# A fused attention and mixer kernel: its order taken from a list plan instead of generators and tile pools

## The chip, the cores and the metric

The kernel runs on one core of a Trainium2 chip. The metric is the device time of one execution in microseconds (us). The engines are TensorE (PE, with PEld for its weight loads), VectorE (DVE), ScalarE (ACT), GpSimd (POOL) and SyncE (SP). POOL issues the loads, which convert float32 to bfloat16 on the way; SP issues the stores.

## The reference

There are 8 batches of 576 positions, 8 heads of 64, and a model width of 512.

```python
scores = scale * q @ k^T + slope[h] * -(i - j)        # where 0 <= i - j < 128, else -1e9
x = softmax(scores) @ v                               # heads side by side: [8, 576, 512]
u = x + (relu(x^T @ w_tok1) @ w_tok2)^T               # token mix: 576 -> 256 -> 576
out = u + relu(u @ w_ch1) @ w_ch2                     # channel mix: 512 -> 1536 -> 512
```

## The kernel before, in words

576 positions are four blocks of 128 and a remainder of 64. Two batches form a pair `pr`: blocks 0 to 3 are the even batch, 4 to 7 the odd one, and the two remainders share block 8, `TAIL`, one in partitions 0 to 63 and one in 64 to 127. A block has a q, a k and a v tile, 1,024 rows of 64 numbers each (512 for half of TAIL).

Attention of a block: `transposes` (L199, copied by DVE at L205 into `qkT`), `scores` (L225: 64-row matmuls, even and odd heads in the two row halves of the array), an Exp on ACT (L234), `mask` on DVE (L245), `values` (L266, reciprocal L269, normalising multiply L271) into `xb`. A window of 128 makes each block need its own keys and those of the block before.

`token_mix` of a batch: two accumulations `t1` over the batch's four blocks (L314) and its 64 remaining rows (L318, 64-row matmuls), relu on ACT (L332), then for each block `ht` (L348), an add on DVE (L349), `ut` transposes (L354) and a copy (L360). For odd batches there is also TAIL, whose weights `W2t` are padded with zeros to 128 columns for each of its halves. `channel_mix`: 12 `ct` groups of four matmuls (L446) with relu on ACT (L448), for odd batches 3 `cx` groups for TAIL (L455), then for each block an accumulation `o2` of 12 matmuls (L464) in four pieces, an add (L468) and a store.

The order: `opening` writes out batch 0's attention and token mix by hand, with matmuls on zeros (`spin`) between. After that `interleave` alternates channel mix b with `side(b + 1)`, which is the attention and token mix of the next batch, by costs in nanoseconds that generators yield:

```python
interleave(main, other, 0.78 if b else 1.4)
drain(other)
```

So `side` advances 0.78 of what the channel mix does, and what is left of it is drained. The tile scheduler orders the other engines and POOL's and SP's queues. POOL's order at the start is: blocks 0 to 3 and half of TAIL, W1, W2, WC1 in four parts, WC2 in four parts, W2t, blocks 4 to 7, the other half of TAIL, and from there one block for each `transposes` of a later one. PSUM has 8 banks: the scores take two pairs, `ps_o` has one (tp, ot, ut), `ps_m` three (t1, ht, ct, cx, o2).

Of the kernel before, what the change touches and what calls it, by code (L numbers as in the profile page):

```python
# [12 lines left out]
F32 = mybir.dt.float32  # L13


@with_exitstack
def kernel(
# [37 lines left out]
    ld = ctx.enter_context(tc.tile_pool(name="ld", bufs=12))  # L55
    tpool = ctx.enter_context(tc.tile_pool(name="tp", bufs=8))
    ppool = ctx.enter_context(tc.tile_pool(name="pp", bufs=3))
    small = ctx.enter_context(tc.tile_pool(name="small", bufs=4))
    xpool = ctx.enter_context(tc.tile_pool(name="xp", bufs=2))
    rpool = ctx.enter_context(tc.tile_pool(name="rp", bufs=2))  # L60
    opool = ctx.enter_context(tc.tile_pool(name="op", bufs=3))
    rawp = ctx.enter_context(tc.tile_pool(name="raw", bufs=2))
    PS = bass.MemoryType.PSUM
    ps_s = [ctx.enter_context(tc.tile_pool(name=f"ps_s{e}", bufs=1, space=PS)) for e in range(2)]
    ps_o = ctx.enter_context(tc.tile_pool(name="ps_o", bufs=1, space=PS))
    ps_m = ctx.enter_context(tc.tile_pool(name="ps_m", bufs=3, space=PS))

    ident = const.tile([P, P], BF16, name="ident")

    dist = const.tile([P, 2, P], F32, name="dist")  # L70

    NV = 14
    vring = [const.tile([P, H, D + 1], BF16, name=f"v{i}") for i in range(NV)]
    made = {"v": 0}
# [9 lines left out]
    loaded = {}  # L84

    def tiles(pr, blk):
        got = {"q": ld.tile([P, H, D], BF16, name="qld", tag="qld"),
               "k": ld.tile([P, H, D], BF16, name="kld", tag="kld"),
               "v": vring[made["v"] % NV]}
        made["v"] += 1  # L90
        loaded[pr, blk] = got
        return got

    def fetch(got, parts):
        for name, t in (("q", q), ("k", k)):
            for b, s0, n, p0 in parts:
                nc.gpsimd.dma_start(out=got[name][p0 : p0 + n, :, :], in_=rows(t, b, s0, n))  # L97
        for b, s0, n, p0 in parts:
            nc.gpsimd.dma_start(out=got["v"][p0 : p0 + n, :, 0:D], in_=rows(v, b, s0, n))  # L99


    ORDER = [0, 1, 2, 3, 7, TAIL, 4, 5, 6]
    todo = [(pr, blk) for pr in range(1, B // 2) for blk in ORDER]

    def load_next(n):
        for _ in range(n):
            if todo:
                key = todo.pop(0)
                fetch(tiles(*key), parts_of(*key))


    zero = const.tile([P, DM], BF16, name="zero")
    nc.vector.memset(zero[:, :], 0.0)
    for t in vring[0:5]:
        nc.vector.memset(t[:, :, D : D + 1], 1.0)
    raws = []
    for name, t, eng in (("q", q, nc.sync), ("k", k, nc.scalar)):
        raw = rawp.tile([P, H, D], F32, name="raw", tag="raw")
        eng.dma_start(out=raw[:, :, :], in_=rows(t, 0, 0, P))
        raws.append(raw)  # L120
# [7 lines left out]

    tiles(0, 0)
    tiles(0, 1)  # L130
    for name, t in (("q", q), ("k", k)):
        nc.gpsimd.dma_start(out=loaded[0, 1][name][:, :, :], in_=rows(t, 0, P, P))
    for blk in (0, 1):
        nc.gpsimd.dma_start(out=loaded[0, blk]["v"][:, :, 0:D], in_=rows(v, 0, blk * P, P))
    for blk in (2, 3):
        fetch(tiles(0, blk), parts_of(0, blk))
    last = tiles(0, TAIL)
    for name in ("q", "k"):
        nc.vector.memset(last[name][R:P, :, :], 0.0)
    nc.vector.memset(last["v"][R:P, :, 0:D], 0.0)  # L140
    fetch(last, parts_of(0, TAIL)[0:1])
    for t in vring[5:]:
        nc.vector.memset(t[:, :, D : D + 1], 1.0)


    masks = [const.tile([P, 4, 2, P], BF16, name=f"mask{e}") for e in range(2)]
    maskt = [const.tile([P, 4, 2, P], BF16, name=f"maskt{e}") for e in range(2)]
    for e in range(2):
        for i, h in enumerate(HEADS[e]):
            nc.scalar.activation(out=masks[e][:, i, :, :], in_=dist[:, :, :], func=ACT.Exp,  # L150
                                 scale=-float(slopes[h]))

    def tail_masks():

        for e in range(2):
            for i in range(2):
                nc.vector.tensor_copy(out=maskt[e][:, :, 0, i * R : (i + 1) * R],
                                      in_=masks[e][:, :, 0, 0:R])
            nc.vector.tensor_copy(out=maskt[e][:, :, 1, :], in_=masks[e][:, :, 1, :])
            nc.vector.memset(maskt[e][0:R, :, 1, R:P], 0.0)  # L160


    W1 = const.tile([P, NC + 1, DTOK], BF16, name="W1")
    W2 = const.tile([P, NJ, NC * P], BF16, name="W2")
    W2t = const.tile([P, 2, NJ, P], BF16, name="W2t")
    WC1 = const.tile([P, NCB, DCH], BF16, name="WC1")
    WC2 = const.tile([P, NHT, DM], BF16, name="WC2")
    nc.vector.memset(W2t[:, 0, :, R:P], 0.0)
    nc.vector.memset(W2t[:, 1, :, 0:R], 0.0)

    def load_weights():
        nc.gpsimd.dma_start(
            out=W1[:, 0:NC, :], in_=moe_w_tok1[0 : NC * P, :].rearrange("(c p) n -> p c n", p=P)
        )
        w2 = moe_w_tok2.rearrange("(j p) s -> p j s", p=P)
        for i in range(2):
            nc.gpsimd.dma_start(out=W1[i * R : (i + 1) * R, NC, :], in_=moe_w_tok1[NC * P : S, :])
        nc.gpsimd.dma_start(out=W2[:, :, :], in_=w2[:, :, 0 : NC * P])
        w = moe_w_ch1.rearrange("(j p) h -> p j h", p=P)
        for x in range(4):  # L180
            hs = slice(x * DCH // 4, (x + 1) * DCH // 4)
            nc.gpsimd.dma_start(out=WC1[:, :, hs], in_=w[:, :, hs])
        w = moe_w_ch2.rearrange("(j p) c -> p j c", p=P)
        for x in range(4):
            js = slice(x * NHT // 4, (x + 1) * NHT // 4)
            nc.gpsimd.dma_start(out=WC2[:, js, :], in_=w[:, js, :])
        for i in range(2):
            nc.gpsimd.dma_start(out=W2t[:, i, :, i * R : (i + 1) * R], in_=w2[:, :, NC * P : S])


    qkT = {}
    xs = {}

    def transposes(pr, blk, copy):
        got = loaded[pr, blk]
        tp = ps_o.tile([P, 2 * NHP, P], BF16, name="tp", tag="o")
        for i, t in enumerate(("q", "k")):
            for hp in range(NHP):
                nc.tensor.transpose(  # L199
                    tp[:, i * NHP + hp, :],  # L200
                    got[t][:, 2 * hp : 2 * hp + 2, :].rearrange("p h d -> p (h d)"),
                    ident[:, :],
                )
        t = tpool.tile([P, 2 * NHP, P], BF16, name="qkT", tag="qkT")
        copy(out=t[:, :, :], in_=tp[:, :, :])  # L205
        qkT[pr, blk] = t

    def scores(pr, blk, half=None):


        tail = blk == TAIL
        c0, c1 = (0, P) if half is None else (half * R, (half + 1) * R)
        first = 0 if tail or blk % NC else 1
        me = qkT[pr, blk]
        sp = [ps_s[e].tile([P, 4, 2, P], F32, name=f"sp{e}", tag="s") for e in range(2)]
        work = [(1, blk, c0, c1)]
        if tail:
            work += [(0, (j + 1) * NC - 1, j * R, (j + 1) * R) for j in range(2)
                     if half is None or half == j]
        elif not first:  # L220
            work += [(0, blk - 1, 0, P)]
        for i in range(4):
            for kind, kb, a, z in work:
                for e in range(2):
                    nc.tensor.matmul(  # L225
                        sp[e][:, i, kind, a:z],
                        lhsT=qkT[pr, kb][e * D : (e + 1) * D, NHP + i, :],
                        rhs=me[e * D : (e + 1) * D, i, a:z],
                        start=True, stop=True,
                    )  # L230
        pb = []
        for e in range(2):
            pe = ppool.tile([P, 4, 2, P], BF16, name=f"pe{e}", tag=f"pe{e}")
            nc.scalar.activation(out=pe[:, :, first:, c0:c1], in_=sp[e][:, :, first:, c0:c1],  # L234
                                 func=ACT.Exp, scale=scale)
            pb.append(pe)
        return pb

    def mask(blk, pb, half=None):
        tail = blk == TAIL  # L240
        c0, c1 = (0, P) if half is None else (half * R, (half + 1) * R)
        first = 0 if tail or blk % NC else 1
# [78 lines left out]
    def token_mix(b):  # L321
# [6 lines left out]
        for j in range(NJ):  # L328
            t1 = ps_m.tile([P, DM], F32, name="t1", tag="m")
            for c in range(NC + 1):  # L330
                mix_in(t1, half, j, c, xb)
# [216 lines left out]
```

## Time and profile before

| | |
|---|---|
| median of 3 runs | 337.15 us (335.84 to 337.27) |
| profiled execution | 337.96 us, span 336.2 us |
| PE busy | 310.6 us, 92% of the span |
| DVE, ACT, POOL busy | 173.3, 137.4, 110.4 us |
| mean granted PE clock | 0.971 |
| loads through POOL's queue | 115,648 packets, 17.7 MB |

Times are counted from the first instruction of the span. "Busy" sums an engine's instructions; matmul ends are modelled. The clock is the share of full speed that was granted to PE. In a timeline row the columns are start, duration, engine, line, operation, what it writes and reads, the count, and in brackets the idle time ahead of it with what ended it.

### The profile page before, as it was taken

To read this page: it belongs to the slowest core of one execution; us is meant where nothing else is said; L and a number is where in the kernel's file an instruction comes from. 1 tells how busy PE (TensorE), PEld (TensorE's weight loads), DVE (VectorE), ACT (ScalarE), POOL (GpSimd) and SP (SyncE) were. 2 spreads that over 40 slices of the span, in tenths; PEclk is the share of its full clock that TensorE was granted. 3 is DMA by queue.
4 is the path that set the end of the run, shared out by engine and by line. 5 is a ranking of instruction groups with operands and counts; after the bars stand their busy time and mean duration, and the time that the engine had idled before them with its cause. 6 is when DMAs were issued, how large, how long until landed. Compare 5 with 4: busy or idle time off the path is not lost.

```text
span 336.2 us, 6518 instructions
## 1 busy us (share of the span) xinstructions
PE 310.6 (92%) x2693; PEld 163.1 (49%) x2739; DVE 173.3 (52%) x394; ACT 137.4 (41%) x210; POOL 110.4 (33%) x141
## 2 busy tenths in 40 slices
PE   8877998677999999999999999999999999999993
PEld 3543454324655555455564555455664555455541
DVE  4865057643665646474656547464756447361021
ACT  5523754112764037503863047404772057304600
POOL 9873698899774033303572000000000000000000
PEclk9977999957999999999999999999999999999998
DMA  9999999999999269914999220011000120011022
GB/s 126 142 180 205 147 146 171 186 131 149 133 87 98 65 117 72 66 51 93 77 82 79 96 62 3 0 65 62 2 2 25 71 64 0 2 62 62 2 88 69
DMA packets 123005, 28.08 MB, mean 84 GB/s; under 512 B 113888, under 2 KB 118368, under 8 KB 122976
## 3 DMA queue, kind: packets, MB, share of 16 engines
q0 software_dynamic: 115648, 17.70, 74.2%
q1 hardware_dynamic: 6288, 9.70, 8.6%
q8 instruction: 21, 0.34, 0.4%
q10 hardware_dynamic: 1040, 0.26, 0.4%
q14 instruction: 8, 0.07, 0.1%
HBM read 35.91 MB, written 9.44 MB: 135 GB/s over the span
## 4 chain that ended last, share of the span: by engine, by line
PE 83%; DVE 7%; POOL 3%; issue 2%; ACT 2%; DMA 2%; POOLq 0%
PE o L464 28%; PE ct L446 22%; PE ot L266 6%; PE sp L225 5%; PE tp L199 5%; PE ht L348 5%; PE t L314 4%; PE ut L354 3%; PE cx L455 2%; DVE xb L271 2%; DVE pe L245 2%; DMA kld<-in_k_dram 2%; PE t L318 1%; ACT pe L234 1%; PE hh L422 1%
## 5 line engine op out<-in xcount | busy, mean ns | idle before, releaser
L448 ACT ACTIVATE r<-ct 128x512 bf16<-128x512 f32 x96 | 56.2, 601 | 124.5 <-PE ct L446 124.5
L464 PE MATMUL o<-WC,r 128*128 128x512 bf16 x367 | 94.3, 379 | 2.1 <-DVE ob L468 0.8
L446 PE MATMUL ct<-uT,WC 128*128 128x512 bf16 x366 | 93.3, 382 | 2.0 <-issue 0.8
L234 ACT ACTIVATE pe<-sp 128x1024 bf16<-128x1024 f32 (+1 forms) x74 | 63.2, 906 | 26.6 <-PE sp L225 26.6
L464 PEld LDWEIGHTS <-r 128*128 128x128 bf16 x384 | 35.2, 98 | 37.9 <-issue 4.6
L446 PEld LDWEIGHTS <-WC 128*128 128x128 bf16 x384 | 34.2, 98 | 30.5 <-issue 1.3
L97 POOL DMA_DIRECT2D qld<-in_q_dram x38 | 33.2, 875 | 46.3 <-PE tp L199 37.7
L468 DVE TENSOR_TENSOR ob<-o,ub 128x512 f32<-128x512 f32 x36 | 24.8, 689 | 45.6 <-PE o L464 44.2
L245 DVE TENSOR_TENSOR pe<-pe,mask 128x1024 bf16<-128x1024 bf16 (+1 forms) x66 | 39.5, 613 | 8.6 <-ACT pe L234 8.0
L205 DVE COPY qkT<-tp 128x1024 bf16<-128x1024 bf16 x37 | 25.6, 691 | 34.6 <-PE tp L199 34.6
L99 POOL DMA_DIRECT2D v<-in_v_dram x38 | 33.0, 883 | 15.8 <-PE ot L266 6.6
L266 PE MATMUL ot<-v,pe 128*128 128x65 bf16 (+1 forms) x552 | 29.8, 196 | 5.7 <-DVE xb L271 4.9
L97 POOL DMA_DIRECT2D kld<-in_k_dram x38 | 33.4, 883 | 5.0 <-DMA WC<-in_moe_w_ch_dram 3.5
L349 DVE TENSOR_TENSOR ub<-ht,xb 128x512 bf16<-128x512 f32 x32 | 21.6, 688 | 25.8 <-PE ht L348 25.4
L266 PEld LDWEIGHTS <-pe 128*128 128x128 bf16 (+1 forms) x552 | 21.8, 100 | 23.5 <-DVE xb L271 17.2
L271 DVE TENSOR_TENSOR xb<-ot,rt 128x256 bf16<-128x256 f32 (+1 forms) x74 | 31.4, 424 | 2.5
L269 DVE RECIPROCAL rt<-ot 128x4 f32<-128x4 f32 (+1 forms) x74 | 13.3, 179 | 25.1 <-PE ot L266 24.6
L225 PE MATMUL sp<-qkT 64*128 64x128 bf16 (+1 forms) x552 | 22.4, 214 | 2.3 <-DVE qkT L205 2.2
L225 PEld LDWEIGHTS <-qkT 64*128 64x128 bf16 x552 | 15.8, 94 | 17.4 <-DVE qkT L205 16.7
L314 PE MATMUL t<-xb,W 128*128 128x512 bf16 x59 | 18.6, 404 | 0.4 <-issue 0.4
L348 PE MATMUL ht<-r,W 128*128 128x512 bf16 x53 | 17.2, 416 | 0.4 <-ACT r L332 0.3
L360 DVE COPY uT<-ut 128x512 bf16<-128x512 bf16 x28 | 11.8, 422 | 8.2 <-PE ut L354 8.2
(67 smaller groups left out, 208.9 us busy)
## 6 DMA issues: line engine op xcount, KB each, us to landing
out_dram<-ob SPq DMA_DIRECT2D x32, 256.0 KB, 2.0
v<-in_v_dram POOLq DMA_DIRECT2D x32, 128.0 KB, 4.9
qld<-in_q_dram POOLq DMA_DIRECT2D x31, 128.0 KB, 4.8
kld<-in_k_dram POOLq DMA_DIRECT2D x31, 128.0 KB, 4.8
WC<-in_moe_w_ch_dram POOLq DMA_DIRECT2D x8, 384.0 KB, 11.9
out_dram<-ob SPq DMA_DIRECT2D x8, 128.0 KB, 2.3
qld<-in_q_dram POOLq DMA_DIRECT2D x8, 64.0 KB, 4.5
kld<-in_k_dram POOLq DMA_DIRECT2D x8, 64.0 KB, 4.2
```

The lines of the kernel that those rows point to most:

```text
L97: nc.gpsimd.dma_start(out=got[name][p0 : p0 + n, :, :], in_=rows(t, b, s0, n))
L99: nc.gpsimd.dma_start(out=got["v"][p0 : p0 + n, :, 0:D], in_=rows(v, b, s0, n))
L225: nc.tensor.matmul(sp[e][:, i, kind, a:z], lhsT=qkT[pr, kb][e * D : (e + 1) * D, NHP + i, :], rhs=me[e * D : (e + 1) * D, i, a:z], start=T ...
L234: nc.scalar.activation(out=pe[:, :, first:, c0:c1], in_=sp[e][:, :, first:, c0:c1], func=ACT.Exp, scale=scale)
L245: nc.vector.tensor_tensor(out=pb[e][:, :, first:, c0:c1], in0=pb[e][:, :, first:, c0:c1], in1=mk[:, :, first:, c0:c1], op=ALU.mult)
L266: nc.tensor.matmul(ot[to, i, :], lhsT=l, rhs=r, start=m == 0, stop=m == len(mms) - 1, skip_group_check=True)
L271: nc.vector.tensor_tensor(out=x4[r0:r1, :, e, :], in0=ot[r0:r1, :, 0:D], in1=rt[r0:r1, :, :].broadcast_to([r1 - r0, 4, D]), op=ALU.mult)
L314: nc.tensor.matmul(t1[:, :], lhsT=W1[:, c, j * P : (j + 1) * P], rhs=xb[:, half * NC + c, :], start=c == 0, stop=False)
L348: nc.tensor.matmul(ht[:, :], lhsT=l, rhs=r, start=n == 0, stop=n == len(mms) - 1)
L446: nc.tensor.matmul(ct[:, :], lhsT=WC1[:, cb, t * P : (t + 1) * P], rhs=uT[:, cb, :], start=cb == 0, stop=cb == NCB - 1)
L448: nc.scalar.activation(out=r2[:, t, :], in_=ct[:, :], func=ACT.Relu)
L464: nc.tensor.matmul(o2[:, :], lhsT=l, rhs=WC2[:, t, :], start=t == 0, stop=t == NHT - 1)
```

## The change

Every step becomes an operation of a `Plan`: an engine, a cost in nanoseconds, a rank, and the buffers that it makes, adds to, rewrites or reads. Buffers are placed in rings of fixed tiles. `plan.run()` is a list schedule at build time: at each turn it takes, over all engines, the operation that can start earliest (rank, then number, breaks ties), places its buffers in the slot that comes free first, and moves the engine's clock on. POOL's operations keep the order in which they were written. Then `emit` sorts everything by its planned start and writes it out; all five engines keep that order. In predicted gaps of PE over 500 ns in the first 60 us it puts matmuls on zeros into a bank that the plan has free.

- PSUM: four banks in one ring for tp, ot, ut, t1, ht, ct, cx and o2; the scores keep their two pairs.
- POOL's order: WC1, then blocks 4 to 7, W2t, the other half of TAIL, then WC2, then the later pairs.
- Ranks: `side(0)` ahead of everything, then `side(1)`, then channel mixes in turn, with `side(b + 1)` spread over 0.93 of channel mix b. Several batches' steps can mix.
- Opening: no order by hand; all four adds and all four uT copies go to DVE (ACT and an identity matmul had half).
- Token mix: `HOLD` makes the first t1 matmul wait for the batch's third block. TAIL's rows are copied by DVE into the other half of partitions (`xt`), so that t1 for j = 0 and j = 1 take different row halves; both `t1` banks are then held until TAIL's x is there.
- W2t loses its zero padding: 64 columns, written to output partitions 0 to 63 and 64 to 127.

The diff, cut to its core:

```diff
+SEM = 40.0
+SPREAD = 0.93
+class Plan:
...
+    def dma(self, emit, descs, packets, makes=(), rewrites=(), order=None):
+        o = self.op("POOL", 550 + 0.33 * descs, emit, 0, makes=makes, rewrites=rewrites,
+                    order=order or self.slot())
...
+    def run(self):
...
+        free = {"PE": 1500.0, "ACT": 5600.0, "DVE": 1600.0, "POOL": 2000.0, "SP": 1300.0}
+        server, lanes, sent = SERVER, [], 0
...
+                    if e == "POOL" and len(lanes) >= 8:
+                        t = max(t, lanes[-8])
+                    key = (t if t > free[e] + 1e-6 else free[e], o.rank, o.n)
...
+            if e == "PE":
+                slow = 2.0 if t < WARM else 1.0
+                if t > free[e]:
+                    self.gaps.append((free[e], t))
+                    t += 60.0
+                o.t0 = t
+                free[e] = t + o.cost * slow
+                o.done = free[e] + 165.0
...
+            else:
+                o.t0 = t
+                free[e] = t + o.cost
+                server = max(server, t + 1000) + o.packets * PACKET
+                o.done = server + 1500
...
+WARM = 9000.0
+HOLD = 2
+FILL = 60000.0
+SERVER = 4000.0
+PACKET = 0.86
...
-    ps_s = [ctx.enter_context(tc.tile_pool(name=f"ps_s{e}", bufs=1, space=PS)) for e in range(2)]
-    ps_o = ctx.enter_context(tc.tile_pool(name="ps_o", bufs=1, space=PS))
-    ps_m = ctx.enter_context(tc.tile_pool(name="ps_m", bufs=3, space=PS))
+    ctx.enter_context(tc.manual_schedule(engines={E.PE, E.Activation, E.DVE, E.Pool, E.SP}))
+    plan.ring("bank", [psum.tile([P, DM], F32, name=f"bank{i}") for i in range(4)])
...
+    lw1 = weights([(W1[:, 0:NC, :], w1, 512, 700)] +
+                  [(W1[i * R : (i + 1) * R, NC, :], moe_w_tok1[NC * P : S, :], 64, 100) for i in range(2)])
+    lw2 = weights([(W2[:, :, :], w2[:, :, 0 : NC * P], 256, 600)])
...
+        lc1 += weights([(WC1[:, :, hs], c1[:, :, hs], 512, 2100)]) * (NHT // 4)
+    for blk in (4, 5, 6, 7):
+        for name in "qkv":
+            load(name, 0, blk, parts_of(0, blk))
+    lw2t = weights([(W2t[:, :, :], w2[:, :, NC * P : S], 256, 300)])
+    later = [plan.slot() for _ in "qkv"]
...
+        lc2 += weights([(WC2[:, js, :], c2[:, js, :], 384, 2100)]) * (NHT // 4)
...
+        plan.op("DVE", 260, lambda: dve_.tensor_copy(out=xt()[far, :], in_=xb()[own, TAIL, :]), rank(0),
+                makes=xt, reads=[(xb, (TAIL, tk))])
...
+                rd = [(xb, (blk, None))] + ([(xb, (blocks[HOLD], None))] if c == 0 else [])
...
+            for j, rs, rhs in ((0, own, xb()[own, TAIL, :]), (1, far, xt()[far, :])):
+                pe_.matmul(t1[j]()[:, :], lhsT=W1[rs, NC, j * P : (j + 1) * P], rhs=rhs, start=False, stop=True)
...
+                            pe_.matmul(ht()[i * R : (i + 1) * R, :], lhsT=W2t[:, j, :],
+                                       rhs=r1s[2 * pr + i]()[:, j, :], start=j == 0, stop=j == NJ - 1)
...
+            side(nb, along(base - 1e5, 1.0, 1.0) if b == 0 else along(base, SPREAD * n, tot))
...
+    plan.run()
+    plan.emit(spin)
```

## The prediction

> **What bounds the kernel now.** I read the forty slices first, then TensorE's busy time by stage, then the rows where a stage loses time.
>
> ```profile
> PE   8877998677999999999999999999999999999993
> ...
> PEclk9977999957999999999999999999999999999998
> DMA  9999999999999269914999220011000120011022
> ```
>
> A slice is 8.4 us. From slice 10 on, TensorE (PE) is full and at full clock. Before that it has holes, and the granted clock drops twice. The DMA engines are busy through just this early part. The second view cuts the span where batch 0's channel mix starts (32.57), where batch 2's starts (121.33) and where the last channel mix runs alone (304.8); its row at 62 lies inside the second stretch.
>
> ```profile
> 0.00:32.57 32.57, 25.24 (x242) 13.30 (x246) 20.57 (x67) 14.66 (x24) 24.31 (x38) 0.90 1.49 162
> 32.57:121.33 88.76, 80.09 (x708) 41.96 (x721) 45.25 (x101) 34.21 (x51) 61.88 (x74) 0.94 1.76 133
> 62.00:81.30 19.30, 12.75 (x93) 6.13 (x89) 9.10 (x21) 2.32 (x5) 18.13 (x23) 0.73 2.18 151
> 121.33:304.80 183.47, 179.46 (x1592) 94.78 (x1618) 103.31 (x221) 79.56 (x120) 24.22 (x29) 1.00 0.39 51
> 304.80:336.20 31.40, 25.84 (x154) 13.05 (x154) 4.15 (x6) 8.96 (x15) 0.00 (x0) 0.96 0.15 51
> ```
>
> The first two numbers are the stretch and PE's busy time; the clock is the third from the end. Stretch 2 idles 8.7 us (88.76 − 80.09) and loses about 5.2 more to the clock (27% of 19.3). What is left, 74.9 us, is work. Stretch 3 idles only 4.0 us in 183.5. So what there is to win lies ahead of 121 us. The hole at 62 to 81 is a serial end: channel mix 0 is used up, and batch 1's token mix has nothing to alternate with, as PE's rows show.
>
> ```profile
> 64.61 0.42 PE L266 MATMUL ot<-v,pe 128*128 128x65 bf16 x8 [1.79 <-DVE xb L271]
> 65.77 0.44 PE L266 MATMUL ot<-v,pe 128*64 128x65 bf16 x8 [0.73 <-DVE xb L271]
> ...
> 68.13 1.01 PE L318 MATMUL t<-xb,W 64*128 64x512 bf16 x2 [0.74 <-DVE xb L271]
> ```
>
> Why was batch 1 so late? Its loads queue on POOL behind all of WC1 and WC2, and POOL itself waits until a WC part has landed:
>
> ```profile
> 23.66 0.72 POOL L188 DMA_DIRECT2D W2t<-in_moe_w_tok_dram  x1 [0.86 <-DMA WC<-in_moe_w_ch_dram]
> ...
> 30.79 0.87 POOL L97 DMA_DIRECT2D kld<-in_k_dram  x1 [2.42 <-DMA WC<-in_moe_w_ch_dram]
> ```
>
> Block 4's k is issued at 30.79 and takes 9.3 us to land (the DMA view of 27 to 34 us):
>
> ```profile
> kld<-in_k_dram POOLq DMA_DIRECT2D x1, 128.0 KB, 9.3
> ```
>
> So it is there at 40.1.
>
> **The change, part by part.**
>
> *Opening, to 32.57.* Its loads keep their order, so block TAIL's k lands at 17.6 as now (its transposes wait for it at 17.63). From the copy at 18.06 VectorE (DVE) owes: that copy 0.69, unit 3's masks 1.28, its two norms with reciprocals 1.2, TAIL's masks 0.75 and norms 1.2, together 5.1, so 23.2. Before, it stood idle 2.11 us at 24.09 because PE had eight token matmuls queued ahead of TAIL's values, at half clock. The plan lets those slip and fills predicted gaps with spins. Then: the new half-block copy 0.3, tails 0.4, relu 0.65, first ht and its landing 0.6, and now all four adds (0.65 each, pipelined) and four copies (0.4 each) on DVE, where ACT had taken half: 4.2. Sum 29.4, so channel mix 0 can start at 29.5 instead of 32.57. Bounds: 27.5 if adds and copies interleave without a gap and the tail comes off earlier, 33 if spins run at half clock.
>
> *Loads reordered.* Blocks 4 to 7 now go ahead of WC2. WC1's four parts land as now; the row at 30.79 is the fourth. Two loads at POOL's pace of 0.87 put block 4's k at about 32.2, 8 us earlier. The plan, however, believes otherwise: up to that load it counts 10 whole and 3 half loads (1,024 packets each, halves 512), 1,500 for W1 and W2, 8,400 for WC1 and 2,048 for the block's q and k, 23.7 thousand at 0.86 ns; from 4.0, plus 1.5, plus about 1 where POOL's issue holds the server up, that makes 27, some 5 us too early. By its own model channel mix 0 starts near 27 too (its TAIL is 2.4 us early), so PE's frozen order has the transposes of block 4 at the very start of it, and nothing may overtake. Cost: PE idles from 29.5 to 32.2, 2.7 us. From there loads follow each other as the plan thinks, since its 0.88 us per load matches the 0.87 of the rows, so the lag stays and costs no second time. WC2 lands some 13 us later than now, from about 45; until then PE has channel mix 0's first half (10.3) and batch 1's side (12).
>
> *The clock after that stall.* The row at 62 shows 0.73 with no PE gap above 1.79 us, so a 2.7 us hole counts. That row lost 5.2 us to several holes; I take a third of it for this one, 1.7, with 0 and 5.2 as bounds.
>
> The Trainium skill ("TensorE: Matmul & The Clock Gate", "What's actually happening") gives the drop after an idle window of about 3.4 us; by that rule the stall costs nothing and the sum would be 1.7 us lower, but the row at 62 speaks against it.
>
> *Channel mix 0, batch 1's side, channel mix 1, batch 2's side* (stretch 2) become one pool of work, ordered by rank. Of 88.8 us, 74.9 are work. From 32.2: 74.9, less 1.0 for the padding below, plus 1.7 for the clock, plus 1.6 of waits at stretch 3's rate (4.0/183.5 × 74), is 109.4, where now it is 121.3. **Gain 11.9.**
>
> *Padding dropped.* The token mix's two 64-row matmuls now sit in different row halves and banks. Their price now shows here:
>
> ```profile
> 138.90 0.38 PE L314 MATMUL t<-xb,W 128*128 128x512 bf16 x1
> 139.21 0.39 PE L318 MATMUL t<-xb,W 64*128 64x512 bf16 x1
> 139.53 1.04 PE L314 MATMUL t<-xb,W 128*128 128x512 bf16 x4
> ```
>
> Starts of full matmuls are 0.216 apart; into and out of the 64-row form it is 0.31 and 0.32, so each crossing costs 0.1. Twice per batch becomes once, and two matmuls run as one pair (score pairs do: 16 of 128 columns in 0.62, where 8 transposes of 128 columns take 0.61): 0.2 + 0.21 = 0.41 per batch, 0.8 in stretch 2 and 2.05 for sides 3 to 7. The extra DVE copy (0.26) is covered: DVE is 56% busy there; uncovered it would add 0.3 per batch. The tail's ht goes from four full matmuls to four of 64 columns, two at a time. No row has such a pair at 512 columns. Bounds per pair of batches: +0.43 if they overlap free of charge, −0.2 if they don't and still pay two crossings. I take 0.23 (overlap, with crossings, as the score rows have it): 0.2 in stretch 2, 0.7 after.
>
> The Trainium skill ("TensorEngine Tiling (Array Packing)", "Key Properties") speaks against this part: changing the tiling mode drains TensorE. It gives no figure; taken as wiping the overlap out, the sum would be 0.9 us higher.
>
> *Stretch 3.* Four pooled banks instead of one plus three end waits like "PEld L266 <- DVE xb L271", 17.2 us in total on the weight side. But PE itself idles 4.0 us here, so no more can go. I take half, 2.0 (bounds 4.0 gained and 20 lost, see rivals). With 2.75 of padding: **gain 4.75.**
>
> *The last stretch* has one channel mix, the last add and the store on both sides: 0.
>
> Sum: −16.7 on the profiled execution of 337.96 (span 336.2 and 1.76 around it) gives 321.3; the median, 337.15, lies 0.8 below that execution: **320.5**.
>
> **The rivals.**
>
> *The plan holds fully.* PE has enough ranked work ahead of block 4, so there is no stall, no clock drop and no wait: 29.5 + 73.9 = 103.4, a gain of 17.9, and 2.75 + 4.0 after. 337.15 − 24.7 = 312.5. For it: 10 us of channel mix is ready by 29.5. Against: the 5 us by which its packet model is early.
>
> *The plan orders, but the chip is late.* Opening as now (32.6), 4 us of stalls, as much clock loss as now (5.2), waits 1.6: 32.6 + 73.9 + 10.8 = 117.3. Gain 4.0 + 4.75: 328.4. For it: every landing time in the plan after 15 us is too early. The changed order then changes little.
>
> *Slower: the banks.* Two t1 banks are now held together until TAIL's x is there, and an o2 bank is held over its four spaced pieces. One bank is left for ct, cx, ot, tp. A ct turn in one bank is 0.86 of matmuls, then its relu (rows: first matmul 32.57, relu 33.63 to 34.23), 1.7 in all instead of 0.86. At 24 ct per pair of batches that is up to 20 us a pair; over 2.5 pairs it eats the whole 16.7 and passes 1.7 us (0.5%) when 9 of 24 are caught. With 12 caught: 25.2 − 16.7, 345.7. Against: the token matmuls have late ranks, when o runs instead of ct.
>
> **How the numbers follow.** Forecast 0.54 (own range 313 to 326, from the opening's 27.5 to 33 and the clock's 0 to 5), plan fully 0.13, late chip 0.16, no change 0.03, banks 0.14. Half a percent, 1.7 us, is about what a measurement of this kernel can tell from no change. Faster 0.83, same 0.03, slower 0.14. The range 308 to 332 takes in the first three: 308 is the full plan with an opening at 27.5 and 2 us of bounds, 332 the late chip with one more half-clock stretch. About 0.2 is left out.
>
> **What would show it.** Right: block 4's k is issued before WC2; PE waits there for it, near 30 to 32; the hole at 62 to 81 is gone; batch 2's channel mix starts near 109; L318's kind of matmul starts as pairs; the last 31 us are the same. Wrong: PE idle in many places in steady state with ACT or DVE as releasers (banks), half clock during the opening, or waits for WC2 after 45.

## The result, and the profile after

| | before | changed |
|---|---|---|
| median | 336.96 us (4 runs) | 312.55 us (312.07 to 314.59, 4 runs) |
| ratio | | 0.9293, 95% interval 0.9246 to 0.9339 |
| profiled execution, span | 337.96, 336.2 us | 312.54, 310.6 us |

The change makes the kernel 7.1% faster. The forecast was 320.5 with a range of 308 to 332; the rival "the plan holds fully" had 312.5.

The slices of the page, changed kernel (one is 7.8 us here):

```profile
PE   6686999999999999999999999999999999999992
...
PEclk9999999999999999999999999999999999999999
DMA  9999999999999979119996110110001110110013
```

PE is full from slice 4 on instead of 10, and no slice shows the half clock. The stretches, cut where channel mix 0, 2 and 7 begin (31.69, 104.52, 278.47; before: 32.57, 121.33, 304.8), with columns as in the prediction:

```profile
0.00:31.69 31.69, 22.57 (x249) 12.21 (x253) 21.61 (x66) 12.42 (x20) 26.06 (x39) 1.00 1.61 152
31.69:104.52 72.83, 72.14 (x706) 40.80 (x718) 45.73 (x109) 33.59 (x51) 59.17 (x73) 1.00 2.02 166
62.00:81.30 19.30, 19.14 (x215) 11.61 (x217) 9.88 (x23) 12.33 (x19) 16.91 (x20) 1.00 2.14 170
104.52:278.47 173.95, 172.14 (x1583) 94.32 (x1611) 101.26 (x225) 79.42 (x120) 24.69 (x30) 1.00 0.42 55
278.47:310.60 32.13, 26.59 (x157) 13.39 (x158) 4.11 (x6) 8.96 (x15) 0.00 (x0) 0.98 0.15 50
```

The opening gives 0.9 us, the second stretch 15.9 (88.76 to 72.83), the third 9.5 (183.47 to 173.95), and the last costs 0.7, since a little of channel mix 6 is now left when 7 begins. The old hole at 62 to 81 is full. One hole is left, ahead of the second stretch; PE's rows show it:

```profile
28.12 0.40 PE L555 MATMUL bank<-ident,ub 128*128 128x128 bf16 x4 [0.20 <-DVE ub L547]
30.40 0.40 PE L405 MATMUL bank<-ident,q 128*128 128x128 bf16 x4 [1.88 <-DMA q<-in_q_dram]
31.24 0.40 PE L405 MATMUL bank<-ident,k 128*128 128x128 bf16 x4 [0.44 <-DMA k<-in_k_dram]
```

and the chain between 15 and 33 us says what it hangs on, block 4's k, issued at 20.07, ahead of WC2 (columns: start, duration, what):

```profile
20.07 11.13 DMA k<-in_k_dram
31.19 0.05 issue
31.24 0.40 PE bank L405 x4
```

It lands at 31.2, 9 us earlier than before.

### The profile page after: what moved, and what is told of

It is laid out like the page before. It is cut to its first block, busy times and chain, and to the rows that moved or that the text cites. A ratio compares the mean times of both kernels' runs of the same rounds, so it can differ in the third digit from the quotient of the medians.

```text
span 310.6 us, 6527 instructions
## 1 busy us (share of the span) xinstructions
PE 293.4 (94%) x2690; PEld 160.7 (52%) x2738; DVE 172.7 (56%) x404; ACT 134.4 (43%) x206; POOL 109.9 (35%) x140
## 4 chain that ended last, share of the span: by engine, by line
PE 84%; POOL 6%; DMA 4%; DVE 2%; ACT 1%; issue 1%; POOLq 0%; ACTq 0%
PE bank L630 30%; PE bank L602 24%; PE bank L475 5%; PE wide L436 5%; PE bank L405 5%; PE bank L504 4%; PE bank L538 4%; DMA k<-in_k_dram 4%; PE bank L616 3%; PE bank L555 2%; POOL v L337 1%; POOL q L337 1%; DVE pe L450 1%; POOL k L337 1%; POOL WC L342 1%
## 5 line engine op out<-in xcount | busy, mean ns | idle before, releaser
L607 ACT ACTIVATE r<-bank 128x512 bf16<-128x512 f32 x96 | 57.1, 599 | 100.7 <-PE bank L602 94.3
L630 PE MATMUL bank<-WC,r 128*128 128x512 bf16 x366 | 95.5, 379 | 0.9
L602 PE MATMUL bank<-uT,WC 128*128 128x512 bf16 x358 | 92.5, 379 | 1.0
L444 ACT ACTIVATE pe<-wide 128x1024 bf16<-128x1024 f32 (+1 forms) x74 | 63.1, 906 | 10.1 <-PE wide L436 10.1
L637 DVE TENSOR_TENSOR ob<-bank,ub 128x512 f32<-128x512 f32 x36 | 24.8, 691 | 72.8 <-PE bank L630 72.5
L337 POOL DMA_DIRECT2D q<-in_q_dram x39 | 33.8, 873 | 30.3 <-PE bank L405 26.7
L337 POOL DMA_DIRECT2D k<-in_k_dram x39 | 33.9, 874 | 5.4 <-DMA WC<-in_moe_w_ch_dram 3.5
L410 DVE COPY qkT<-bank 128x1024 bf16<-128x1024 bf16 x37 | 25.3, 683 | 13.6 <-PE bank L405 13.3
L483 DVE TENSOR_TENSOR xb<-bank,rt 128x256 bf16<-128x256 f32 (+1 forms) x74 | 30.8, 421 | 1.8
L475 PE MATMUL bank<-v,pe 128*128 128x65 bf16 (+1 forms) x552 | 28.0, 195 | 1.0 <-DMA v<-in_v_dram 0.6
L520 ACT ACTIVATE r<-bank 128x512 bf16<-128x512 f32 x15 | 8.2, 595 | 43.1 <-PE bank L511 43.1
```

The lines of the kernel that those rows point to most:

```text
L337: nc.gpsimd.dma_start(out=buf()[p0 : p0 + n, :, 0:D], in_=rows(src, b, s0, n))
L410: dve_.tensor_copy(out=t().rearrange("p a b -> p (a b)"), in_=tp().bitcast(BF16))
L444: act_.activation(out=pb[e]()[:, :, lo:, c0:c1_], in_=wide(e)[:, :, lo:, c0:c1_], func=ACT.Exp, scale=scale)
L475: pe_.matmul(view()[a:z, i, :], lhsT=pb[e]()[:, i, kind, a:z], rhs=vb()[:, h, :], start=m == 0, stop=m == len(mms) - 1, skip_group_check=True)
L483: dve_.tensor_tensor(out=x4[r0:r1_, :, e, :], in0=view()[r0:r1_, :, 0:D], in1=rt()[r0:r1_, :, :].broadcast_to([r1_ - r0, 4, D]), op=ALU.mult)
L602: pe_.matmul(ct()[:, :], lhsT=WC1[:, cb, t * P : (t + 1) * P], rhs=uT()[:, cb, :], start=cb == 0, stop=cb == NCB - 1)
```

## The experiments

All were timed against the kernel before; ratios are to it. "Channel mix 2" below is the start of its first relu in the profile, 122.29 before and 105.58 in the changed kernel; a "pair" is the time from there to channel mix 4's, two batches, 74.81 and 71.20.

**1. The loads' order undone in the plan** (`a_wc2_first`): the block that makes `lc2` goes ahead of `for blk in (4, 5, 6, 7)`.

> The changed kernel with one part undone: WC2's four loads go ahead of blocks 4 to 7 again, and the plan is drawn up anew for it. Theory (the early gain needs loads and order together): block 4's k lands near 39.5 instead of 31.2, channel mix 0 starts near 29 without a stall but batch 1's side ends some 5 us later, with a hole before channel mix 1: 316 to 320 us. Rival 1 (the loads' order alone makes the early gain): nearly all of the early 16.7 is lost, 327 us or more. Rival 2 (the order of steps alone; the loads would hide under channel mix 0 anyway): 310 to 313, the stall of 2.3 us gone.

Measured: 318.79 us, ratio 0.947 (0.9441 to 0.9499). The theory's number. The price is all early: channel mix 2 at 110.28 (4.7 later), the pair unchanged at 71.2. The hole is not where I put it: PE waits 2.4 us for block 4's q between 30 and 40, and a half-clock stretch follows; between 60 and 72 just 1.1 us are idle.

```profile
30.00:40.00 10.00, 7.14 (x38) 3.29 (x38) 1.26 (x6) 4.18 (x7) 5.84 (x7) 1.00 1.81 180
40.00:50.00 10.00, 9.90 (x104) 5.24 (x103) 4.82 (x13) 6.46 (x10) 8.61 (x12) 0.83 2.16 136
```

**2. The loads' order alone, in the kernel before** (`b_loads`): WC2's and W2t's loads move out of `load_weights`.

```diff
+    def load_wc2():
...
+            nc.gpsimd.dma_start(out=WC2[:, js, :], in_=w[:, js, :])
...
     for blk in (4, 5, 6, 7):
         fetch(tiles(0, blk), parts_of(0, blk))
+    load_wc2()
```

> The kernel before with one part done alone: WC2's four loads go behind blocks 4 to 7, the order of steps stays. Theory: batch 1's side is held back by the order, since all 12 ct groups come first; only the two waits for loads at 50 and 55 (1.0 us) go: 335 to 337 us, and the hole at 62 to 81 stays. Rival 1: 322 to 328. Rival 2: 337.

Measured: 338.72 us, ratio 1.0102 (1.005 to 1.0155); the profiled span was 335.2. No gain, somewhat worse than the theory allowed. The hole stays: from 60 to 82 PE is busy for 15.4 us at a clock of 0.84.

**3. The order of steps alone** (`b_early`): the 12 leading ct groups and the barrier go, and the share is 0.78 for batch 0 too.

```diff
-        if b == 0:
-            for _ in range(NHT):
-                next(main)
-            tc.no_sync_barrier()
-        interleave(main, other, 0.78 if b else 1.4)
+        interleave(main, other, 0.78)
```

> The kernel before with the order of steps changed alone: batch 1's side alternates with channel mix 0 from its first ct group on, at a share of 0.78 as for the other batches; loads as before. Theory: PE now waits in its queue for block 4 until 40 and for blocks 5 to 7 after it; the hole moves ahead instead of going: 333 to 342 us. Rival 1: 337. Rival 2: 322 to 328.

Measured: 334.12 us, ratio 0.9936 (0.9918 to 0.9953). The hole moves ahead, as the theory had it (PE's waits between 28 and 60, then total, times, longest):

```profile
PE tp L199 <- DMA qld<-in_q_dram: 8.4, 1, 8.4
```

**4. Both, in three versions.** The first two did not do what they set out to.

> The kernel before with both: WC2's loads behind blocks 4 to 7, and batch 1's side alternating from the first ct group on at 0.78; still generators and tile pools. Theory: block 4 is there near 32, the hole at 62 to 81 and its half clock go: 323 to 329 us, most of the early gain without a list plan. Rival 1: the same as the loads alone. Rival 2: the same as the order alone.

Measured: 333.75 us, ratio 0.9926 (0.9901 to 0.9951), a miss. The tile scheduler still issued TAIL's other half after WC2, and PE stood there:

```profile
55.86 0.61 PE L202 MATMUL tp<-ident,qld 128*128 128x128 bf16 x4 [6.65 <-DMA qld<-in_q_dram]
```

> The kernel before with batch 1's side alternating from the first ct group on at 0.78, and WC2's loads behind blocks 4 to 7 and behind TAIL's other half as well, which the earlier version of this left behind WC2 (PE stood 6.65 us for TAIL's q at 55.9). Still generators and tile pools. Theory (the early gain needs loads and order together, the list plan is only one way to it): the wait for TAIL and the half clock after it go, 325 to 329 us. Rival (only the list plan's placing gets it): 332 to 335, with another wait in its place.

Measured: 333.38 us, ratio 0.9881 (0.9842 to 0.992). A miss again, for the same reason: writing the lines in another order did not move the queue (TAIL's q issued at 46.88, PE waiting 7.58 until 55.48). The third version fixes POOL's order as the changed kernel does:

```diff
+    with tc.manual_schedule(engines={E.Pool}):
         fetch(last, parts_of(0, TAIL)[1:2])
+        load_wc2()
         load_next(2)
```

> The kernel before with batch 1's side alternating from the first ct group on at 0.78 and POOL's queue now really in the changed kernel's order: blocks 4 to 7, TAIL's other half, then WC2 (in the two earlier versions TAIL's half was still issued after WC2, at 46.9 in the second, and PE stood some 7 us for it). Theory (loads and order together make the early gain, by whatever means): TAIL lands near 41, no wait at 48 to 55, 325 to 329 us. Rival (with the tile pools' banks another wait takes its place): 332 to 335.

Measured: 325.12 us, ratio 0.967 (0.9645 to 0.9694). This is the theory's number, and the second stretch, here from 31.0, has no hole and no clock loss left (the second row is steady state):

```profile
31.00:108.64 77.64, 76.20 (x721) 40.04 (x721) 45.13 (x102) 33.42 (x51) 61.21 (x74) 1.00 2.06 158
108.64:292.10 183.46, 181.88 (x1620) 94.81 (x1619) 103.27 (x221) 79.57 (x120) 24.25 (x29) 1.00 0.39 51
```

Channel mix 2 starts at 109.70. So 12.6 of the 16.7 us that the change gains up to there need no plan: the loads and one loop in the right order, and a POOL queue that keeps them. The other 4.1 were not split further. Steady state is the old one, 74.80 a pair.

**5. The padding undone in the plan** (`a_padding`).

```diff
-                            pe_.matmul(ht()[i * R : (i + 1) * R, :], lhsT=W2t[:, j, :],
+                            pe_.matmul(ht()[:, :], lhsT=W2t[:, i, j, :],
...
-            for j, rs, rhs in ((0, own, xb()[own, TAIL, :]), (1, far, xt()[far, :])):
+            for j in range(NJ):
+                pe_.matmul(t1[j]()[:, :], lhsT=W1[own, NC, j * P : (j + 1) * P], rhs=xb()[own, TAIL, :],
```

> The changed kernel with one part undone: W2t is padded again (four full ht matmuls for TAIL), both t1 tails use the batch's own row half one after the other, and the copy to the other half is gone; the plan is drawn up anew. Theory (PE-bound, each matmul counts): 0.3 x 4 + 0.4 x 8 = 4.4 us more, 315.5 to 318. Rival (the plan hides it behind waits that are there anyway): 312 to 314.

Measured: 315.99 us, ratio 0.9372 (0.9333 to 0.941), 3.4 us more than the changed kernel (2.4 between the two profiled executions). The pair is 71.83, so what this run undoes is 0.63 of the 3.6 us that a pair gained. It doesn't undo all of the prediction's padding part: its plan still puts a batch's two 64-row matmuls one behind the other, so the 64-row form is entered once per batch and not twice:

```profile
127.05 0.60 PE L509 MATMUL bank<-xb,W 64*128 64x512 bf16 x2
```

At the prediction's 0.2 per batch that is about 0.4 of a pair (an estimate from its rows at 138.90 to 139.53). The other 2.6 are something else.

**6. The banks tied again in the plan** (`a_banks_tied`).

```diff
-    plan.ring("bank", [psum.tile([P, DM], F32, name=f"bank{i}") for i in range(4)])
+    plan.ring("bank", banks[0:3])
+    plan.ring("o", banks[3:4])
```

The ring "o" serves tp, ot and ut.

> The changed kernel with the four shared PSUM banks tied again as before: one for tp, ot and ut, three for t1, ht, ct, cx and o2; the plan is drawn up anew for that. Theory (steady state's gain beyond the padding, 2.4 us per pair of batches, comes from any step taking any bank): 318 to 321. Rival (it comes from the order of the list, which can work around tied banks): 312 to 314.5.

Measured: 339.18 us, ratio 1.005 (1.0013 to 1.0088). Far beyond either number: all is lost. Channel mix 0's first relu comes at 45.65 (32.75 in the changed kernel). That part is no fair picture of the old banks, since the hand-written opening of before took `ot` and `ut` from the three banks, and here they are tied to the one from the start. In steady state the old tie holds, and the pair takes 75.6: the side ends with four ut transposes in one bank and nothing to put between (three of them are shown), and PE waits 2.5 us a pair for their copies:

```profile
152.41 0.40 PE L557 MATMUL bank<-ident,ub 128*128 128x128 bf16 x4
153.32 0.38 PE L557 MATMUL bank<-ident,ub 128*128 128x128 bf16 x4 [0.52 <-DVE uT L563]
154.64 0.38 PE L557 MATMUL bank<-ident,ub 128*128 128x128 bf16 x4 [0.94 <-DVE uT L563]
```

This shows that this list needs the shared banks, not that shared banks are the gain.

**7. The banks shared in the kernel before** (`b_pool`): `ps_o` goes, `ps_m` gets 4 buffers, and tp, ot and ut take their banks there.

> The kernel before with one part done alone: one pool of four PSUM banks for tp, ot, ut, t1, ht, ct, cx and o2 instead of one and three; order and loads as before. Theory (shared banks make most of steady state's gain beyond the padding): the pair of batches takes 72.3 to 73.3 us instead of 74.8, 329 to 333 in all. Rival (the list's order makes it): 74.3 to 75 a pair, 335 to 338.

Measured: 330.93 us, ratio 0.9839 (0.9813 to 0.9866). The total is the theory's and its reason is not: the pair takes 75.3 us, 0.5 more than before. The gain is early (channel mix 0's relu at 30.57 instead of 33.63, channel mix 1's at 72.34 instead of 81.15). So my theory on the banks fell, and in steady state the rival (74.3 to 75) is the nearer one.

**8. All of it without a plan** (`b_all`): experiment 4's third version with 7's banks.

> The kernel before with all of these: loads in the new order, batch 1's side from the first ct group on, four shared banks; padding as before, no list plan. Theory (these parts add up; the plan is one way to them): 318 to 324 us, within some 5 us of the changed kernel with padding (316.0). Rival (only the list plan gets it): 329 or more.

Measured: 327.89 us, ratio 0.974 (0.9706 to 0.9775). The parts don't add up: shared banks cost 2.8 us on top of 325.12. Of the 2.3 between the two profiled executions, 1.1 come ahead of channel mix 2 (110.83 instead of 109.70) and 1.2 behind it (75.3 a pair). Its 329 was the rival's line, and 327.9 is nearer to that.

**9. The spins left out** (`a_no_spins`): `FILL = 0.0`.

> The changed kernel without the matmuls on zeros in predicted gaps; nothing else differs. Theory (they keep the clock full through the opening, where PE has little work): half clock until some time after the channel mix starts, 2 to 5 us more, 314.5 to 317.5. Rival (the opening waits for loads and VectorE, its matmuls have room at half clock): 312 to 313.5.

Measured: 312.71 us, ratio 0.9271 (0.9234 to 0.9308): no difference in time, and yet the theory is right on the clock. The first transposes take 0.61 instead of the changed kernel's 0.40, and so do those at 16.79; only from about 25 us on are they at 0.40. The opening ends some 3 us later for it, with ut at 30.62 and 31.22 instead of 27.53 and 28.12, and most of what it loses is taken out of the wait for block 4, which is gone (channel mix 2 comes at 106.47, 0.9 later):

```profile
5.37 0.61 PE L405 MATMUL bank<-ident,q 128*128 128x128 bf16 x4 [5.37 <-DVE q L354]
...
16.79 0.61 PE L405 MATMUL bank<-ident,q 128*128 128x128 bf16 x4 [1.32 <-DMA q<-in_q_dram]
...
31.22 0.40 PE L555 MATMUL bank<-ident,ub 128*128 128x128 bf16 x4 [0.20 <-DVE ub L547]
31.55 0.38 PE L405 MATMUL bank<-ident,q 128*128 128x128 bf16 x4
```

So the spins keep the clock full, and here that is hidden behind a load. In experiment 10's kernel, which has no such wait, they should count; that was not tried.

**10. A better load model in the plan** (`a_model`).

```diff
-PACKET = 0.86
+PACKET = 0.9
...
-    lw1 = weights([(W1[:, 0:NC, :], w1, 512, 700)] +
+    lw1 = weights([(W1[:, 0:NC, :], w1, 512, 2400)] +
```

and likewise W2 600 to 2400, the small parts of W1 100 to 300, WC parts 2100 to 2250.

> The changed kernel with its plan's load model put nearer to the landings measured (0.9 ns a packet, W1 and W2 counted as 2,400 packets each, their small parts 300, WC parts 2,250), so that the plan expects block 4 near 31 instead of 27. Theory (the stall at 28.5 to 31.2 is the price of a load model that is 4 us early): the plan puts ct groups ahead of block 4's transposes, 2.0 to 2.5 us less, 309.5 to 311. Rival (PE then waits for the loads a little later instead): 312 to 313.5.

Measured: 310.07 us (309.58 to 310.57), ratio 0.9219 (0.9196 to 0.9242). The theory's number, and the fastest version here. PE now has three ct groups to do until block 4 is there:

```profile
28.60 2.75 PE L602 MATMUL bank<-uT,WC 128*128 128x512 bf16 x12 [0.92 <-DVE uT L561]
31.19 0.39 PE L405 MATMUL bank<-ident,q 128*128 128x128 bf16 x4
```

and from there until channel mix 7 the profile shows no idle time at all:

```profile
28.60:101.80 73.20, 73.20 (x726) 40.99 (x726) 46.11 (x109) 34.09 (x51) 61.06 (x74) 1.00 2.12 170
101.80:275.75 173.95, 173.95 (x1612) 94.33 (x1611) 101.28 (x225) 79.42 (x120) 24.69 (x30) 1.00 0.42 55
```

## Why the prediction was right, and where it was off

The forecast gain was 16.7 us; between the profiled executions it was 25.4. The order of events was right: loads first, a stall for block 4, the old hole gone. The sizes were short by some 9 us, 4.9 in the second stretch and 4.1 in steady state.

*Opening and stall: right.* Predicted: uT done at 29.5, then PE idle until block 4's k at 32.2. Measured: the last ut starts at 28.12, PE stands for 1.88 and 0.44 us, the k lands at 31.2. That the stall comes from the plan's early load model, not from the loads, is shown by experiment 10, where telling the plan better numbers took 2.5 us off (312.55 to 310.07).

*The clock after the stall: the term of 1.7 us was wrong for this kernel.* The profile shows 1.00 until the last channel mix. It was no invention: with a wait of 2.4 us in `a_wc2_first` the next 10 us ran at 0.83, which is just 1.7 us. Similar holes cost it in one kernel and not in the other. The length of one wait doesn't tell them apart; how busy PE was over a fixed stretch of 3.41 us nearly does. In the fourteen profiles every recorded half-clock stretch ahead of the last channel mix is 3.41 us long, or two or three times that. So I divided each trace, from its first clock record to its last channel mix, into pieces of 3.41 us. At full clock, the 11 pieces in which PE was less than half busy were all followed by half clock, and of the 1,105 in which it was over 62% busy none was. In between it was 10 of 25. The wait of 2.4 us fell mostly into one piece (first two rows, `a_wc2_first`: PE busy for 1.37 of 3.41, then half clock). In the changed kernel the pieces count from 5.35, and a boundary at 29.24 split the wait of 1.88. The emptier piece (third row) was busy for 1.75 of 3.41, which is 51%; the next piece kept the full clock, though in this range it need not have:

```profile
36.53:39.94 3.41, 1.37 (x12) 0.85 (x13) 0.46 (x1) 0.00 (x0) 2.19 (x3) 1.00 2.42 155
39.94:43.35 3.41, 3.41 (x16) 1.09 (x15) 0.28 (x2) 1.81 (x4) 3.21 (x5) 0.50 2.43 155
...
29.24:32.65 3.41, 1.75 (x13) 0.86 (x15) 1.12 (x4) 0.00 (x0) 2.64 (x4) 1.00 2.43 155
```

So what a given hole costs depends on its neighbours and on where the boundaries fall. The rule that I set aside, a drop after an idle window of about 3.4 us (the Trainium skill, "TensorE: Matmul & The Clock Gate", "What's actually happening"), has the length as these traces do; but the window need not be idle, 40% busy was little enough.

*The second stretch: mechanism right, 4.9 us short* (batch 2's channel mix predicted at 109.4, measured at 104.5). 1.7 is the clock, 1.0 the k that landed at 31.2 instead of 32.2, 0.9 the waits (0.7 idle, 72.83 − 72.14, instead of 1.6). The other 1.3 I had counted as work; most likely they are waits that the busy time hides, as in the next point, but that was not shown for this stretch.

*Steady state: the term that was mis-sized.* I wrote that "PE itself idles 4.0 us here, so no more can go", took 2.0, and added 2.75 for padding. The third stretch and the last together gave 8.85 (from channel mix 2's relu to the end, 213.9 to 205.05). Padding is 1.66 of it by the profiles (206.71 with padding, from the same point), and the saved crossings, which that run keeps, are about 1.0 more (0.2 for each of five batches). So the term for waits should have been about 6.2. The idle of the busy table was the wrong measure twice over. Part of it isn't idle: the page of before counts 2,693 matmuls for 2,739 weight loads, so some 46 records are missing. `b_loads_early3` has the same steady state with none missing, and idles 1.6 there (183.46 − 181.88). And a wait of a weight load hides under the modelled ends of the matmuls ahead of it. The starts of the matmuls show it. I took the steps between starts in one pair, less the shortest that such steps are in these traces (0.216 us behind a matmul of 512 columns, 0.056 behind 128, 0.025 to 0.03 within scores and values, about 0.1 more at a crossing), and set the new overlapping pairs aside. What is left over is 3.4 us in `b_loads_early3` (pair 74.80) and 0.9 in `a_model` (pair 71.21, no record missing either). The difference, 2.5 a pair, is 6.2 for the two and a half pairs. What they waited for stands in the waits of PEld. One pair of batches, before (196.14 to 270.96; total, times, longest):

```profile
PEld L266 <- DVE xb L271: 3.9, 10, 0.7
PEld L225 <- DVE qkT L205: 3.4, 8, 0.4
```

and the same pair after (176.78 to 247.99), where the largest that has a releaser on another engine are

```profile
PEld L436 <- DVE pe L450: 0.8, 2, 0.4
...
PEld L436 <- DVE xb L483: 0.4, 1, 0.4
```

The first of before is the single `ps_o` bank, the second scores that follow their copy too closely. Shared banks alone take the first away and leave the second (`b_pool`, 188.88 to 264.16):

```profile
PEld L224 <- DVE qkT L204: 3.2, 7, 0.7
```

and they add waits of PE for ACT's relu, 0.8 us, since tp now takes its turn among the ct banks; in all a pair gets no shorter. In the list's trace both are gone: it takes the bank that is free first and puts the scores where their copy is long done. That neither shared banks alone (`b_pool`) nor this list with tied banks (experiment 6) gets there is shown; which of the ranks, the 0.93 and `HOLD` places the scores so is not. I quoted 17.2 us of just this wait in the prediction and then let the busy time overrule it.

*Padding: right in kind.* TAIL's ht, four full matmuls in 1.03 before, takes 0.62, and the two 64-row matmuls start together:

```profile
126.35 0.39 PE L511 MATMUL bank<-xb,W 64*128 64x512 bf16 x1
126.35 0.39 PE L511 MATMUL bank<-xt,W 64*128 64x512 bf16 x1
...
131.09 0.62 PE L534 MATMUL bank<-r,W2t 128*64 128x512 bf16 x4
```

The prediction had 3.75 in all, 0.8 + 2.05 for the token mix and 0.2 + 0.7 for ht. Of that, 1.4 are the crossings of seven batches, which experiment 5 leaves in place; against the remaining 2.35 it measured 3.4 by median and 2.4 between profiled executions. In steady state the 1.66 and about 1.0 of crossings match the 2.75. The drain that comes with a change of tiling mode (the Trainium skill, "TensorEngine Tiling (Array Packing)", "Key Properties") did not eat the overlap, as the rows above show.

*The rivals.* "The plan holds fully" came out to the microsecond, in part by chance: the stall that it left out was there, and more waits went than it knew of. "The chip is late" (328.4) had the stall right, but only 2.3 us of it, with no clock loss behind it. The banks did not run short: PE has no wait for one in the changed kernel's pair. Their price was real, but for tying them (experiment 6), not for sharing them.

## What to carry to other kernels

Where the time of an engine is to be judged, add up the starts of its instructions, and read the weight loads' waits: a busy share of 98% hid some 3% of waits here. A frozen order is as good as its slowest wrong number; the plan lost 2.5 us to one load model that ran 4 us early, and correcting it from the trace's landings was the cheapest gain of all. Two edits that do little alone (loads earlier 1.0102, consumer earlier 0.9936) can be worth 11 us together, and whether a queue really took the new order must be read in the trace, since twice it had not.

## What I had not expected of the hardware

A wait of 2.3 us cost no clock in the changed kernel and one of 2.4 us cost 1.7 us in another: the emptiest pieces of 3.41 us were 51% and 40% busy, and of all pieces those under 50% alone always brought half clock. The granted clock of a stretch reads 1.00 where the profile has no record of it yet: without the spins it says so from the start, while the transposes take 0.61 instead of 0.40; durations are the safer witness. Two 64-column matmuls over 512 columns ran side by side in one bank (four in 0.62 us) with a weight load of 0.108 each, where a 128-column one takes 0.098.
